# A gated mix of sliding attention and a token MLP on one core: the last 96 MLP features in column tiles, gate logits on VectorE, a shorter last store, and a new order of all queues

## The chip, the cores and the metric

The kernel runs on one core of one Trainium2 chip. The metric is the device time in microseconds of one execution; lower is better. All inputs and the output are bf16 arrays in the chip's memory. The kernel uses five engines, each with an instruction queue that is worked off in order: TensorE (PE) for matrix products, ScalarE (ACT) for exponentials, the GELU and some copies, VectorE (DVE) and GpSimd (POOL) for masks and elementwise work, and SyncE (SP), which issues all transfers.

## What is computed

x has 2048 tokens of 512 channels. The result mixes two branches by a gate of each token. Branch A is attention with 32 heads of 16 channels, in which a token sees itself and the 255 tokens before it. Branch B normalises each token and then mixes along the *tokens*: 2048 tokens to 1376 features, GELU, and back.

```python
g = sigmoid((x * gate_w).sum(-1, keepdims=True))
# A
qkv = (x @ wqkv).reshape(B, S, 3, H, Dh).transpose(2, 0, 3, 1, 4)
scores = einsum("bhqd,bhkd->bhqk", q, k) * (Dh ** -0.5)
mask = (idx[:, None] - idx[None, :] >= 0) & (idx[:, None] - idx[None, :] < 256)
p = softmax(where(mask, scores, -1e9))
a = einsum("bhqk,bhkd->bhqd", p, v).transpose(0, 2, 1, 3).reshape(B, S, D) @ wo
# B
h = layernorm(x)
u = gelu(einsum("bsd,sf->bdf", h, w1) + b1)
b = (einsum("bdf,fs->bds", u, w2) + b2).transpose(0, 2, 1)
return g * a + (1 - g) * b
```

## The kernel before

**Tiling.** Tokens are cut in 16 tiles of 128 (index `t_`) and 4 blocks of 512 (`i`). The kernel is a list of small tasks; each has a name, the engines that can run it, its dependencies, and the buffers that it takes. The names are what the text uses:

- `xtaI.n.g` transposes the first block of x on TensorE (the other three blocks, `xt1` to `xt3`, come transposed by transfer), `xtc` copies the result out.
- `qK_I`, `kK_I`, `vT` are the projections. Each is a chain of matmuls of 512 columns into one of eight banks of PSUM, the memory that TensorE writes; a name with `.0`, `.2` and so on is a pair of matmuls of the chain. `qc`, `kc`, `vc` copy the results out; `qc` multiplies with a parity pattern.
- `sJ.vN`, `sJ.C` are scores of a group of query tokens J into two pairs of banks, `eJ...` the exponentials of them on ScalarE (1024 columns each), `mJ...` the masks on VectorE or GpSimd, `pvJ.N` the products with V, `n1` to `n4` and `nz` the normalisation, which also brings the result back in place of x.
- `bs`, `ba`, `pow`, `h` are the layer norm.
- `uF.N` (F from 0 to 10) is the first half of the MLP: chain F makes 128 features for all 512 channels, with w1 as the weights and h as the 512 moving columns, over 16 token tiles. Chain 10 has the last 96 features. `ubF` adds the bias and copies to `ug`. `gelu` is one task of four instructions over all of `ug`, with two table loads of ScalarE around it.
- `yT.N` is the second half of the MLP plus the attention's output product: 11 matmuls with w2 and 4 with wo into the same bank, 15 in a chain. `fT` scales with 1 - g and adds the bias, `oT` stores. wo's product lands in the same sum since the attention result is scaled by the gate's ratio beforehand. Token tile 15 is cut in two halves of 256 columns, `y15l` and `y15r`, each with an `f` and an `o`.
- `gate0` makes the gate logits of tokens 0 to 511 on TensorE, 16 matmuls with one moving column; `glT` makes the logits of one of the other twelve token tiles on VectorE, with gate_w spread over all partitions (loaded by `gw`). `gatem`, `gatee`, `ez` finish them.

**Order.** Nothing is scheduled by a rule at run time. `PLAN` (L189) lists for each engine the task names in the order of its queue, with the numbers of the buffers taken behind the colon. `arrange` (L85) walks through the lists with costs of its own and fixes from them in which tiling the plain chains run: a chain task is "flexible" (`flex`), and takes 32-column tiles (mode p, four matmuls in place of one, on four column groups of the array at once) or the whole array (mode d), whichever `THEN` (L280) names for the stretch after the last task with a tiling of its own. Scores use row tiles (s), corner scores (c) and some products (h) 64-row or 64-column tiles, the products with V column tiles (p). A change of mode costs TensorE time, so the plan gathers tasks of a mode.

**Lines.** All flexible chains record their matmuls on L670 in `chain` (L653): with w1 and h it is u, with XT and wqkv a projection, with ug and w2 (`wb`) or with wo it is y. L942, L998 and L1042 are scores, L1087 the products with V, L894 the exponentials, L536 masks on GpSimd, L907 and L974 masks on VectorE, L754 the Q copies, L602 and L603 other copies, L802 the gate's matmuls, L822 the logits on VectorE, L438 to L441 `affine`, the eviction of u and y, L1253 and L1255 the GELU, L591 the warm-up of TensorE on zeros, L608 the transposes of x, L1305 the stores. `wb` holds w1 first and w2 later.

Of the kernel before, what the change touches and what calls it, by code (L numbers as in the profile page):

```python
# [78 lines left out]
SWITCH = 0.095  # L79

BLOCK, AHEAD, FETCH, BUSY = 256, 80, 3.6, 3.0
LATENCY = {"PE": 0.22, "ACT": 0.15, "DVE": 0.12, "POOL": 0.15, "SP": 2.0}


def arrange(tasks):  # L85
# [21 lines left out]
    while len(order) < len(tasks):  # L107
# [19 lines left out]
        t.cost = t.engines[e]  # L127
        ins = t.ins
        if e == "PE":
            new = then if t.flex else t.mode  # L130
            if new != mode:
                t.cost += SWITCH
            if t.flex and new == "p":
                t.tiled = True
                ins *= 4
            if t.mode != "d":
                then = "p" if t.name in THEN else "d"
            mode = new
# [52 lines left out]
        warm:3 xta0.0.0:7 xta0.0.1:6 warmb xta0.1.1:4 xta0.1.0:5 q1_0.0:2 k3_0.0:3 k1_0.0:6 q3_0.0:1 k0_0.0:7  # L191
        q3_0.1 q0_0.0:0 k3_0.1 q1_0.1 q1_0.2 k1_0.1 k3_0.2 k0_0.1 q0_0.1 q2_0.0:5 q1_0.3 q0_0.2 q1_0.4 q0_0.3
        k3_0.3 q3_0.2 q0_0.4 k3_0.4 q3_0.3 k2_0.0:4 q2_0.1 k0_0.2 k1_0.2 k1_0.3 k0_0.3 k1_0.4 q2_0.2 q3_0.4 q2_0.3
        k0_0.4 k2_0.1 k2_0.2 k2_0.3 k2_0.4 q2_0.4 s0.v0:62 q3_1.0:0 q3_1.2 k3_1.0:1 k3_1.2 q0_1.0:7 s0.C:42 v1.0:6
        q0_1.2 s-1.C:02 v1.2 v2.0:5 v2.2 s1.v3:02 biast:4 v0.0:7 v0.2 v3.0:5 v3.2 q1_1.0:4 s1.v0:62 v5.0:1 q1_1.2
        gate0:5 v5.2 v14.0:0 s0.v1:62 v13.0:5 k2_1.0:1 v14.2 pv-1.0:6 v10.0:4 k2_1.2 v13.2 s1.v2:26 k2_2.0:0 v10.2
        v15.0:1 v12.0:5 v12.2 v15.2 k2_2.2 pv0.0:2 pv0.1 s1.v1:64 pv0.2 v4.0:1 v4.2 k3_2.0:0 k3_2.2 s2.v1:26 v7.0:5
        v7.2 k0_2.0:4 s1.C:60 k0_2.2 v6.0:3 v6.2 s2.v3:06 k0_1.0:2 k0_1.2 k1_1.0:5 k1_1.2 pv1.0:6 pv1.1 pv1.2
        s2.v0:02 v11.0:4 v11.2 v8.0:5 v8.2 pv1.3 pv1.4 s2.v2:20 q2_1.0:5 v9.0:4 q2_1.2 s2.C:26 v9.2 k1_2.0:1 k1_2.2
        u3.0:0 u3.2 s3.v1:64 u3.4 u3.6 u3.8 s3.C:26 u3.10 u3.12 u3.14 u2.0:1 s3.v2:24 pv2.0:6 pv2.1 u7.0:0 pv2.2  # L200
        pv2.3 u7.2 u2.2 s3.v0:42 u2.4 u7.4 u7.6 s3.v3:46 u7.8 u7.10 u7.12 s4.v0:62 u2.6 u2.8 u2.10 u2.12 u2.14
        s4.v1:24 pv3.0:6 pv3.1 pv3.2 pv3.3 u7.14 u10.0:1 u10.2 s5.v2:42 u10.4 u10.6 u10.8 s4.v3:62 u10.10 q0_2.0:0
# [86 lines left out]
def kernel(  # L289
# [929 lines left out]
    for j in range(-1, NT):  # L1219
# [153 lines left out]
```

## Time and profile before

| | |
|---|---|
| time of the runs, us | 199.88, 200.21, 200.73 (median 200.21) |
| the profiled execution, us | 199.82, of which the span of its instructions 198.1 |
| TensorE matmuls, busy | 193.0 us, 4058 matmuls |
| ScalarE, VectorE, GpSimd busy | 169.0, 156.5, 80.0 us |
| granted TensorE clock | 1.00 |
| transfers | 22.02 MB, 111 GB/s on average |

The profile lists instructions with start, length, engine, line, and the tiles written and read (out<-in); `128*32` are the rows and columns of the array that a matmul uses, `128x512` the partitions and elements of its moving operand. A matmul's length holds its latency, and matmuls are pipelined, so the time that TensorE spends on one is read from its start to the next one's start. The number in brackets is the idle time just before, with what ended it. "PEq" and "SPq" are the sequencers, which issue. A transfer's landing is later than its issue.

### The profile page before, as it was taken

Reading aid. Unit: us, or ns where it says so; the run is one execution under the profiler, and the core shown is the slowest. Engines: PE = TensorE matmul, PEld = TensorE weight load, DVE = VectorE, ACT = ScalarE, POOL = GpSimd, SP = SyncE. Lnnn points to the kernel's source line nnn. Section 1 sums busy time; section 2 is a strip of 40 time slices with the busy share of each in tenths; the row PEclk is TensorE's granted clock in tenths of the full one; section 3 lists DMA queues with packets and bytes.
Section 4 is the critical chain, followed back from the end, with each engine's and each line's share of the span. In section 5 each row is a group of like instructions: output and inputs, shape, how many; then the busy total and the mean of one; then the engine's idle time right before and its main releaser. Section 6 shows DMA issues by size and latency. Waiting matters only on the chain. (4 is left out here: it accounts for less than half of the span.)

```text
span 198.1 us, 9100 instructions
## 1 busy us (share of the span) xinstructions
PE 193.0 (97%) x4058; PEld 93.3 (47%) x4058; DVE 156.5 (79%) x318; ACT 169.0 (85%) x198; POOL 80.0 (40%) x118
## 2 busy tenths in 40 slices
PE   7999999999999999999999999999999999999993
PEld 3643444353635445446543554344445354554572
DVE  1799888879998988986589799636867868869683
ACT  2369999999988996998999899899899989898632
POOL 6394897525344440214223200045069335452310
PEclk9999999999999999999999999999999999999999
DMA  5999798970060000001399770000211220200002
GB/s 156 294 284 232 131 319 278 346 187 0 8 174 18 18 0 3 3 5 32 98 364 367 280 210 3 26 26 30 68 37 58 60 68 22 62 30 30 30 3 83
DMA packets 23189, 22.02 MB, mean 111 GB/s; under 512 B 7566, under 2 KB 21262, under 8 KB 23150
## 3 DMA queue, kind: packets, MB, share of 16 engines
q1 hardware_dynamic: 23150, 21.44, 36.9%
q8 instruction: 32, 0.52, 1.1%
q14 instruction: 7, 0.06, 0.1%
HBM read 15.61 MB, written 2.10 MB: 89 GB/s over the span
## 5 line engine op out<-in xcount | busy, mean ns | idle before, releaser
L894 ACT ACTIVATE et<-ps 128x1024 bf16<-128x1024 f32 (+1 forms) x94 | 89.3, 1015 | 6.1 <-PE ps L942 2.4
L536 POOL TENSOR_SCALAR_AFFINE_SELECT et<-et 128x512 bf16<-128x512 bf16 (+2 forms) x63 | 46.7, 751 | 56.0 <-ACT et L894 40.9
L894 ACT ACTIVATE XT<-ps 128x1024 bf16<-128x1024 f32 (+1 forms) x60 | 58.1, 1011 | 7.3 <-PE ps L942 4.3
L670 PEld LDWEIGHTS <-wb 128*32 128x32 bf16 (+4 forms) x645 | 32.0, 97 | 34.5 <-issue 6.5
L670 PE MATMUL pb<-ug,wb 128*32 128x512 bf16 (+4 forms) x385 | 45.5, 366 | 0.0
L670 PE MATMUL pb<-h,wb 128*128 128x512 bf16 (+2 forms) x260 | 44.5, 381 | 0.0
L536 POOL TENSOR_SCALAR_AFFINE_SELECT XT<-XT 128x512 bf16<-128x512 bf16 (+1 forms) x28 | 20.0, 720 | 46.3 <-ACT XT L894 27.4
L670 PE MATMUL pb<-XT,wqkv 128*128 128x512 bf16 (+2 forms) x190 | 32.4, 372 | 0.4 <-DMA wqkv<-in_A_wqkv_dram 0.3
L1178 DVE STREAM_TRANSPOSE et<-ps 128x1024 f32<-128x1024 f32 (+1 forms) x17 | 20.1, 1183 | 11.9 <-PE ps L1087 11.1
L1087 PEld LDWEIGHTS <-VA 128*32 128x32 bf16 (+1 forms) x1056 | 20.1, 97 | 6.6 <-issue 1.5
L942 PE MATMUL ps<-QZ,KT 32*128 32x256 bf16 (+1 forms) x496 | 23.1, 265 | 0.0
L754 DVE TENSOR_TENSOR QZ<-pb,par 128x1024 bf16<-128x1024 f32 x16 | 19.5, 1221 | 3.2 <-PE pb L670 3.2
L670 PEld LDWEIGHTS <-wqkv 128*128 128x128 bf16 (+1 forms) x190 | 12.7, 98 | 14.6 <-DMA wqkv<-in_A_wqkv_dram 0.5
L670 PE MATMUL pb<-wo,xo 128*32 128x512 bf16 (+2 forms) x152 | 18.1, 375 | 0.0
L1087 PE MATMUL ps<-et,VA 128*32 128x128 bf16 (+2 forms) x624 | 17.9, 218 | 0.0
L942 PEld LDWEIGHTS <-KT 32*128 32x128 bf16 x496 | 7.4, 92 | 20.6 <-ACT et L894 10.7
L670 PE MATMUL pb<-wqkv,XT 128*128 128x512 bf16 (+1 forms) x70 | 16.5, 381 | 0.0
L974 DVE TENSOR_TENSOR et<-et,mask 128x512 bf16<-128x512 bf16 x26 | 13.3, 510 | 2.5 <-ACT et L894 2.4
L441 DVE TENSOR_SCALAR ot<-pb,c,c 128x512 bf16<-128x512 f32 (+1 forms) x11 | 8.6, 785 | 7.4 <-PE pb L670 7.3
L1087 PE MATMUL ps<-XT,VA 128*32 128x128 bf16 (+2 forms) x432 | 13.9, 215 | 0.0
L1087 PEld LDWEIGHTS <-VZ 128*32 128x32 bf16 x832 | 13.2, 98 | 0.7
L770 DVE BATCH_NORM_STATS2 stats<-xo 128x6 f32<-128x512 bf16 x16 | 10.7, 682 | 3.1 <-DMA xo<-in_A_x_dram 3.1
(76 smaller groups left out, 199.4 us busy)
## 6 DMA issues: line engine op xcount, KB each, us to landing
wb<-in_B_w_dram SPq DMA_DIRECT2D x8, 512.0 KB, 8.2
wb<-in_B_w_dram SPq DMA_DIRECT2D x2, 2048.0 KB, 9.2
VZ<-VA SPq DMA_DIRECT2D x26, 70.0 KB, 3.0
xo<-in_A_x_dram SPq DMA_DIRECT2D x3, 512.0 KB, 5.5
out_dram<-ot SPq DMA_DIRECT2D x12, 128.0 KB, 2.4
wb<-in_B_w_dram SPq DMA_DIRECT2D x4, 352.0 KB, 5.8
wqkv<-in_A_wqkv_dram SPq DMA_DIRECT2D x4, 256.0 KB, 5.0
wb<-in_B_w_dram SPq DMA_DIRECT2D x1, 1024.0 KB, 5.3
```

The lines of the kernel that those rows point to most:

```text
L441: return nc.vector.tensor_scalar(out=out_, in0=in_, scalar1=scale, scalar2=bias, op0=ALU.mult, op1=ALU.add)
L536: return nc.gpsimd.affine_select(out=out_, in_=in_, pattern=[[0, n] for n in pattern] + [[step, HB]], compare_op=op, fill=0.0, base=base_, ...
L670: made.append(nc.tensor.matmul(buf(b)[c:z_, c0:c0 + w_], lhsT=lhsT[:, c:z_], rhs=rhs, start=(j == 0), stop=(j == n - 1), skip_group_check= ...
L754: lambda k=k, b=b: nc.vector.tensor_tensor(out=QZ[:, k, :, (i % NQ) * SB:(i % NQ + 1) * SB], in0=buf(b)[:, None, :].to_broadcast([P, 2, SB ...
L770: f"bs{t_}", {"DVE": 0.67}, lambda b=b, t_=t_: nc.vector.bn_stats(buf(b)[:], xo[:, t_, :]),
L894: lambda e=e, b=b, shape=shape: nc.scalar.activation(out=shape(buf(e)), in_=shape(buf(b)), func=ACT.Exp, scale=SCALE),
L942: made.append(nc.tensor.matmul(to[:, :, done:done + m], lhsT=keys(j if x == "A" else j - 1, k)[rows], rhs=q[rows], start=True, stop=True, ...
L974: made.append(nc.vector.tensor_tensor(out=v, in0=v, in1=m.to_broadcast(list(v.shape)), op=ALU.mult))
L1087: return lambda: nc.tensor.matmul(to(), lhsT=v() if callable(v) else v, rhs=buf(e)[rows, col:col + n], start=first, stop=last, tile_positi ...
L1178: lambda: nc.vector.transpose(out=view(buf(tr).bitcast(FP32)), in_=view(buf(o))), [last], takes=[tr], uses=[o],
```

## The change

Five things change together:

1. The last 96 features (chain 10 of u) no longer go through `chain` but through a new function, `narrow`. Of the four column groups of 32, three make 32 features each for 384 of the 512 channels; the fourth makes the remaining 128 channels for all three feature groups, one after the other, next to each other in its part of the bank. The eviction becomes `ub10` (384 columns) and `uc10` (three pieces of 32 partitions by 128).
2. The gate logits of tokens 0 to 511 are made on VectorE as the others are (`NGP` from 1 to 0): `gate0` goes, `gl0` to `gl3` come, and `gw` is loaded earlier.
3. The last token tile is cut in 256, 128 and 128 columns (`y15l`, `y15r`, `y15m`).
4. The zeros of the warm-up are 128 columns, spread by a broadcast read.
5. `arrange` has other costs, and all five lists of `PLAN` and `THEN` are new. The lists are cut here to the stretches that the text speaks of.

```diff
@@ -76,10 +76,29 @@
         self.ready = 0.0
 
 
-SWITCH = 0.095
-
-BLOCK, AHEAD, FETCH, BUSY = 256, 80, 3.6, 3.0
-LATENCY = {"PE": 0.22, "ACT": 0.15, "DVE": 0.12, "POOL": 0.15, "SP": 2.0}
+TURN = {
+    "d": dict(d=0, s=0.100, p=0.100, c=0.098, h=0.100),
+    "s": dict(d=0.116, s=0, p=0.115, c=0.105, h=0.114),
+    "p": dict(d=0.134, s=0.116, p=0, c=0.110, h=0.130),
+    "c": dict(d=0.149, s=0.137, p=0.146, c=0, h=0.137),
+    "h": dict(d=0.150, s=0.137, p=0.135, c=0.140, h=0),
+}
+
+BLOCK, AHEAD, FETCH, BUSY = 256, 80, 3.1, 3.5
+LATENCY = {"PE": 0.21, "ACT": 0.15, "DVE": 0.11, "POOL": 0.12, "SP": 2.0}
+
+
+def cost_of(t, e):
+    c, n = t.engines[e], t.name
+    if e == "PE":
+        return c - 0.02 if t.mode == "s" else c * 0.738 if t.mode == "c" else c
+    if e == "DVE":
+        return max(0.1, c - 0.06)
+    if e == "ACT":
+        return c - 0.085 if n[:2] in ("vc", "kc", "ub") else c - 0.008 if n[0] == "e" else c
+    if e == "POOL" and n[0] == "m" and ".C" in n:
+        return c * 1.14
+    return c
 
 
 def arrange(tasks):
@@ -124,15 +143,15 @@
         assert best is not None, "no task can start: " + ", ".join(q[head[e]].name for e, q in queue.items() if head[e] < len(q))
         start, e, t = best
         head[e] += 1
-        t.cost = t.engines[e]
+        t.cost = cost_of(t, e)
         ins = t.ins
         if e == "PE":
             new = then if t.flex else t.mode
-            if new != mode:
-                t.cost += SWITCH
+            t.cost += TURN[mode][new]
             if t.flex and new == "p":
                 t.tiled = True
                 ins *= 4
+                t.cost += 0.0025 * t.ins
             if t.mode != "d":
                 then = "p" if t.name in THEN else "d"
             mode = new
@@ -188,100 +207,107 @@
...
-        warm:3 xta0.0.0:7 xta0.0.1:6 warmb xta0.1.1:4 xta0.1.0:5 q1_0.0:2 k3_0.0:3 k1_0.0:6 q3_0.0:1 k0_0.0:7
...
-        gate0:5 v5.2 v14.0:0 s0.v1:62 v13.0:5 k2_1.0:1 v14.2 pv-1.0:6 v10.0:4 k2_1.2 v13.2 s1.v2:26 k2_2.0:0 v10.2
...
-        s4.v1:24 pv3.0:6 pv3.1 pv3.2 pv3.3 u7.14 u10.0:1 u10.2 s5.v2:42 u10.4 u10.6 u10.8 s4.v3:62 u10.10 q0_2.0:0
...
-        u9.6 u9.8 s8.v0:04 u8.10 u9.10 u9.12 u8.12 u8.14 s8.v2:06 pv7.0:4 u9.14 pv7.1 pv7.2 pv7.3 s10.v0:02
...
-        q2_3.2 y0.0:7 y0.2 y0.4 y8.0:2 y0.6 y4.2 y0.8 s9.v1:40 y4.4 y8.2 y0.10 y8.4 y0.11 y0.13 s9.v3:40 y4.6 y4.8
...
-        y15l.2 y15r.0:6 y15l.4 y15l.6 y13.10 pv15.0:4 y14.10 pv15.1 pv15.2 y15r.2 y15l.8 y15l.10 y15r.4 y13.11
-        y14.11 y14.13 y13.13 y15r.6 y15r.8 y15l.11 y15l.13 y15r.10 y15r.11 y15r.13
...
-        const zeros bs3:1 xtc0.0.0 bs2:0 ba3 parity bs1:1 ba2 ba1 bs0:0 ba0 qc1_0 bs4:1 qc0_0 ba4 qc3_0 qc2_0 qc3_1
...
-        x0.0 x0.2 wqk0 wqk1 wqk2 wqk3 x1.4 xt1 wv x2.8 bias xt3 x3.12 xt2 vs0 w1_02 w1_03 vs1 w1_22 vs2 gw w1_12
-        w1_23 w1_01 w1_00 w1_10 w1_11 vz2:0 w1_13 vz3:1 vz4:2 vz5:0 w1_20 w1_21 vz6:1 vz8:0 w2_0 vz7:2 w2_1 w2_2
-        vz9:1 wo o0 o4 o8 o7 vz10:2 vs13 o2 o9 o1 vz11:0 vz12:1 o5 o10 vz13:2 o11 vz14:0 o3 o6 o12 o14 o13 o15l
...
+        warm:5 xta0.0.1:4 xta0.0.0:7 warmb xta0.1.0:3 k0_0.0:7 k2_0.0:5 k1_0.0:0 q0_0.0:1 xta0.1.1:4
...
+        q3_1.0:1 q3_1.2 s0.C:26 k2_1.0:0 k2_1.2 v5.0:4 s-1.C:26 v14.0:5 v14.2 v5.2 s1.v3:02 v2.0:6 biast:7
...
+        pv3.2 u0.0:4 u0.2 u2.14 pv3.3 s5.v2:26 u0.4 u10.0:5 u10.2 u10.4 s4.v3:02 u10.6 u10.8 u10.10 u10.12
+        s4.v2:06 u10.14 u0.6 u0.8 s4.C:20 u0.10 u0.12 u0.14 q3_2.0:0 q3_2.2 s6.v0:62 q0_2.0:1 q0_2.2 pv4.0:4
...
+        u8.8 u9.0:6 s8.v1:02 u9.2 u9.4 u9.6 s8.v0:24 u8.10 u8.12 u8.14 s8.v2:04 u9.8 pv7.0:2 u9.10 u9.12
+        q1_3.0:7 u9.14 pv7.1 s10.v0:04 q1_3.2 k2_3.0:6 k2_3.2 pv7.2 pv8.0:4 pv8.1 pv8.2 pv8.3 pv7.3 q3_3.0:0
+        q2_3.0:7 k0_3.0:1 k0_3.2 q3_3.2 q2_3.2 s9.v1:24 y0.0:6 y0.2 y0.4 y0.6 y0.8 y4.0:7 y4.2 y4.4 y4.6
+        s9.v3:04 y4.8 y0.10 y0.11 y0.13 s9.v2:42 y4.10 y4.11 y4.13 y2.0:6 s9.C:40 y2.2 y2.4 y2.6 s9.v0:02
...
+        y14.2 y14.4 y14.6 y14.8 pv15.0:0 pv15.1 pv15.2 y15l.0:2 y13.11 y13.13 y15l.2 y15r.0:3 y15l.4 y15l.6
+        y14.10 y15r.2 y14.11 y14.13 y15l.8 y15l.10 y15l.11 y15r.4 y15l.13 y15r.6 y15r.8 y15r.10 y15m.0:0
+        y15r.11 y15r.13 y15m.2 y15m.4 y15m.6 y15m.8 y15m.10 y15m.11 y15m.13
...
+        zeros const bs1:0 xtc0.0.1 ba1 parity bs3:1 xtc0.1.0 xtc0.1.1 ba3 bs2:0 bs0:1 qc0_0 ba0 ba2 gl1
+        qc1_0 bs6:1 gl0 h3 qc2_0 qc3_0 gl2 gl3 qc3_1 gatem0 ba6 bs4:0 ez0 bs5:1 ba4 biasc bs7:0 ba5 ba7
...
+        x0.0 x0.2 wqk0 wqk1 wqk2 wqk3 gw x1.4 wv xt1 xt3 bias x2.8 xt2 vs0 x3.12 w1_02 vs1 w1_00 w1_11 w1_03
+        vz6:1 vz3:0 vz2:2 vs2 w1_12 w1_10 w1_01 w1_20 w1_13 wo vz4:2 w1_21 w1_23 w1_22 vz7:0 vz5:2 vz8:2
+        w2_0 w2_1 vz11:1 w2_2 o4 vz9:0 o0 o8 vz10:2 o2 o9 o10 o7 vz14:2 vz13:1 vz12:0 vs13 o11 o3 o5 o6 o1
...
@@ -316,7 +342,7 @@
     EPS = 1e-5
     SCALE = DH ** -0.5
     NPE = 1
-    NGP = 1
+    NGP = 0
     NQ = 2
     NK = 3
 
@@ -360,7 +386,7 @@
     ez = sb.tile([P, NT], FP32, name="ez")
 
     EZ = sb.tile([P, 4 * NT], FP32, name="EZ")
-    zeros = ug[:, 0, :]
+    zeros = ug[:, 0, 0:P]
     ident = sb.tile([P, P], BF16, name="ident")
     mask = sb.tile([P, 7, HB], BF16, name="mask")
     par = sb.tile([P, 2], FP32, name="par")
@@ -515,7 +541,7 @@
         nc.vector.memset(half[:], -0.5)
         nc.vector.memset(biases[:], 0.0)
 
-    kz = add("zeros", {"DVE": 0.25}, lambda: nc.vector.memset(zeros, 0.0))
+    kz = add("zeros", {"DVE": 0.16}, lambda: nc.vector.memset(zeros, 0.0))
     k0 = add("const", {"DVE": 0.25}, set_constants)
 
     def identity():
@@ -588,7 +614,10 @@
 
     def warming(n, w):
         return [
-            nc.tensor.matmul(buf(wu)[:, 0:w], lhsT=zeros[:, 0:P], rhs=zeros[:, 0:w], start=True, stop=True)
+            nc.tensor.matmul(
+                buf(wu)[:, 0:w].rearrange("p (a b) -> p a b", b=P), lhsT=zeros,
+                rhs=zeros[:, None, :].to_broadcast([P, w // P, P]), start=True, stop=True,
+            )
             for _ in range(n)
         ]
 
@@ -1232,6 +1261,34 @@
 
 
 
+    NW = 3 * D // 4
+
+    def narrow(fc, mms, deps):
+        b = bank("u")
+        last = None
+        for a in range(0, NT, 2):
+            def emit(a=a):
+                made = []
+                for j in range(a, a + 2):
+                    w, r, rows = mms[j]
+                    for c in range(0, rows, 32):
+                        made.append(nc.tensor.matmul(
+                            buf(b)[c:c + 32, 0:NW], lhsT=w[:, c:c + 32], rhs=r[:, 0:NW], start=(j == 0),
+                            stop=(j == NT - 1), skip_group_check=True, tile_position=(0, c),
+                        ))
+                    for c in range(0, rows, 32):
+                        made.append(nc.tensor.matmul(
+                            buf(b)[rows:P, 4 * c:4 * c + D - NW], lhsT=w[:, c:c + 32], rhs=r[:, NW:D],
+                            start=(j == 0 and c == 0), stop=(j == NT - 1), skip_group_check=True,
+                            tile_position=(0, rows),
+                        ))
+                return made
+            last = add(
+                f"u{fc}.{a}", {"PE": 0.34}, emit, list(deps) if last is None else [last],
+                takes=[b] if a == 0 else [], uses=[] if a == 0 else [b], mode="p", ins=24,
+            )
+        return b, last
+
     ub = []
     m1 = []
     for fc in range(NFC):
@@ -1239,13 +1296,28 @@
         fsz = min(P, F - f0)
         g, w0 = fc // 4, (fc % 4) * P
         mms = [(w1[g][:, t_, w0:w0 + fsz], h[:, t_, :], fsz) for t_ in range(NT)]
-        b, t = chain(f"u{fc}", mms, dw1[g] + hready, "u")
+        if fsz == P:
+            b, t = chain(f"u{fc}", mms, dw1[g] + hready, "u")
+        else:
+            b, t = narrow(fc, mms, dw1[g] + hready)
         m1.append(t)
+        w_ = D if fsz == P else NW
         ub.append(add(
-            f"ub{fc}", {"ACT": 0.66, "DVE": 0.745},
-            lambda b=b, fsz=fsz, fc=fc: affine(ug[:fsz, fc, :], buf(b)[:fsz, :], None, b1c[:fsz, fc:fc + 1]),
+            f"ub{fc}", {"ACT": 0.18 + 0.00094 * w_, "DVE": 0.21 + 0.00104 * w_},
+            lambda b=b, fsz=fsz, fc=fc, w_=w_: affine(
+                ug[:fsz, fc, 0:w_], buf(b)[:fsz, 0:w_], None, b1c[:fsz, fc:fc + 1]
+            ),
             [t, k3], uses=[b],
         ))
+        if fsz < P:
+            def emit_rest(b=b, fc=fc):
+                return [
+                    affine(
+                        ug[c:c + 32, fc, NW:D], buf(b)[fsz:P, 4 * c:4 * c + D - NW], None, b1c[c:c + 32, fc:fc + 1]
+                    )
+                    for c in range(0, fsz, 32)
+                ]
+            ub.append(add(f"uc{fc}", {"ACT": 0.93, "DVE": 0.9}, emit_rest, [t, k3], uses=[b]))
 
     cuts = [(0, 3), (3, 7), (7, NFC - 1)]
 
@@ -1255,7 +1327,7 @@
         made.append(nc.scalar.activation(ug[:rows, NFC - 1, :], ug[:rows, NFC - 1, :], ACT.Gelu_apprx_tanh))
         return made
 
-    gelu = add("gelu", {"ACT": 8.3}, emit_gelu, ub)
+    gelu = add("gelu", {"ACT": 7.0}, emit_gelu, ub)
     gelu_at = [1.3 + 0.15 + 0.43 * (3 if fc < 3 else 7 if fc < 7 else fc + 1) + 0.12 * (1 + (fc >= 3) + (fc >= 7)) + 0.2 for fc in range(NFC)]
 
     def gates():
@@ -1279,7 +1351,7 @@
 
     for t_ in range(NT):
 
-        parts = [("", 0, D)] if t_ < NT - 1 else [("l", 0, D // 2), ("r", D // 2, D)]
+        parts = [("", 0, D)] if t_ < NT - 1 else [("l", 0, D // 2), ("m", D // 2, 3 * D // 4), ("r", 3 * D // 4, D)]
         for tag, c0, c1_ in parts:
             mms = []
             for fc in range(NFC):
```

## The prediction

> **What bounds the kernel now.** The page's first part and the waits of TensorE's matmul queue, in the profiled execution (span 198.1 us):
>
> ```profile
> PE 193.0 (97%) x4058; PEld 93.3 (47%) x4058; DVE 156.5 (79%) x318; ACT 169.0 (85%) x198; POOL 80.0 (40%) x118
> ...
> PE pb L591 <- DVE ug L518: 1.4, 1, 1.4
> PE pb L670 <- DMA wqkv<-in_A_wqkv_dram: 0.3, 1, 0.3
> PE pb L670 <- ACT XT L894: 0.2, 1, 0.2
> ```
>
> The reader is to see a TensorE that works from 1.4 us to 195.0 us and has two waits over 0.1 us after its start. So the time is the sum of what TensorE issues, and I read every price from start to start in its timeline. First the stretch with the last 96 features (128*96 in the rows):
>
> ```profile
> 62.63 1.47 PE L670 MATMUL pb<-h,wb 128*128 128x512 bf16 x6
> 64.04 0.40 PE L942 MATMUL ps<-QZ,KT 32*128 32x256 bf16 x8
> 64.36 1.50 PE L670 MATMUL pb<-h,wb 128*96 128x512 bf16 x6
> 65.79 0.40 PE L942 MATMUL ps<-QZ,KT 32*128 32x256 bf16 x8
> 66.12 0.63 PE L670 MATMUL pb<-h,wb 128*96 128x512 bf16 x2
> ```
>
> Six matmuls of 512 columns take 1.41 us to the next start: 6 x 0.216, and some 0.1 for the change to another tiling of the array. Over all 169 changes in this execution, leaving the untiled mode costs 0.095, leaving column tiles 0.104, and entering any mode 0.010. 96 rows of weights cost as much as 128. Column tiles with 128 columns each, and the gate's matmuls:
>
> ```profile
> 31.21 0.41 PE L1087 MATMUL ps<-et,VA 128*32 128x128 bf16 x16
> 31.45 0.40 PE L1087 MATMUL ps<-XT,VA 128*32 128x128 bf16 x16
> ...
> 23.02 0.54 PE L802 MATMUL pb<-gwc,XT 128*128 128x1 bf16 x16
> 23.43 0.81 PE L670 MATMUL pb<-wqkv,XT 128*128 128x512 bf16 x3
> ```
>
> Sixteen tiled matmuls take 0.235, with the entry: four rounds of four, 0.056 each, new weights for every one. The gate takes 0.41. Then the head and the tail:
>
> ```profile
> 5.26 1.06 PE L608 MATMUL pb<-ident,xo 128*128 128x128 bf16 x8
> 6.57 2.61 PE L670 MATMUL pb<-XT,wqkv 128*128 128x256 bf16 x17 [0.26 <-DMA wqkv<-in_A_wqkv_dram]
> ...
> 193.62 0.81 DVE L441 TENSOR_SCALAR ot<-pb,c,c 128x512 bf16<-128x512 f32 x1 [0.25 <-PE pb L670]
> ...
> 195.04 0.55 DVE L441 TENSOR_SCALAR ot<-pb,c,c 128x256 bf16<-128x256 f32 x1 [0.61 <-PE pb L670]
> ...
> 195.61 0.33 SPq L1305 DMA_DIRECT2D out_dram<-ot  x1
> ```
>
> The first projection starts when wqkv's first block lands (6.57), whatever stands before it. The tail is one eviction, one store, and the end at 198.1. Last, ScalarE around the GELU, where its queue is closed to exponentials:
>
> ```profile
> 111.56 3.88 ACT L894 ACTIVATE XT<-ps 128x1024 bf16<-128x1024 f32 x4 [0.83 <-ACT ez L837]
> 115.47 1.28 ACT L1253 ACT_TABLE_LOAD   x1
> 116.76 4.66 ACT L1253 ACTIVATE ug<-ug 128x1536 bf16<-128x1536 bf16 x3
> ...
> 121.96 1.28 ACT L894 ACT_TABLE_LOAD   x1
> 123.55 1.94 ACT L894 ACTIVATE et<-ps 128x1024 bf16<-128x1024 f32 x2 [0.31 <-PE ps L942]
> ```
>
> From the first table load to the end of the second 7.77 us pass; a following exponential is done about 1.03 later.
>
> **The change, part by part.**
> *Gate on VectorE.* Sixteen matmuls go: -0.40, all on TensorE's path. VectorE gets four logit pairs more, 0.695 + 0.081 each by their rows, some 2.9 us, at about 10 to 18 us into the kernel, between the Q products that s0 to s1 wait for. For it the gate vector's load moves up to just behind the four wqkv loads on SP's queue, past x1, wv, the three transposes and the biases: 128 KB more ahead of each of them. Cover: the fourth wqkv block is in use at 9.02, and the gate vector follows it with half a block's bytes, so by about 9.5; the first logit is due after Q's first product, past 10.5. Cover gone, every us of delay holds VectorE's in-order queue, and s0 behind it.
>
> *u10 in column tiles.* Before: 8 pairs at 0.432 = 3.46. After, per token tile three column tiles run 384 columns (0.216 x 384/512 = 0.162) while the fourth runs three times 128 columns (3 x 0.056 = 0.168): 16 x 0.168 = 2.69, so -0.77. No row of before has unequal widths side by side. Ends: 2.59 if the 384 columns alone count (16 x 0.162), and 5.28 if the 384 and the three 128s follow each other (16 x 0.330). I take 2.69, because the nearest row, the sixteen tiled matmuls, shows four tiles each pacing itself at 0.056 with fresh weights. The eviction becomes one of 384 columns and three of 32 x 128 on VectorE, some 0.6 + 3 x 0.3, beside TensorE.
> The Trainium skill ("TensorE: Matmul & The Clock Gate", Part 3, The mechanism) speaks against it: weight loads overlap running matmuls only where the row groups differ, and these tiles all use every row. With its load time (P/1.2 ns, 27 ns for 32 columns; same page, LDWEIGHTS) my estimate would be 0.056 + 0.027 three times, 0.249 per token tile and 3.98 in all, a loss of 0.5. The sixteen matmuls above have full rows too, and would then take 0.33 where 0.225 was measured, so the row decides. The same section says that matmuls end in the order of issue, which no run here shows for unequal widths.
>
> *Order.* Counted off the two programs' TensorE queues, mode changes go from 169 to 167 in other kinds; priced by kind: -0.24. Tiled and untiled pairs cost the same (0.432), so which pairs are tiled is free. SP's queue is new too. Three blocks of w1's last group, two before, now stand behind vz4, which waits for pv2; before, the two were issued at 55.41 to 56.6 and served u10 at 63.08. One more is 352 KB, 1.2 us at the early 290 GB/s, and u10 stands 1.5 us later: covered. vz9 moves behind o4, the first store, to some 128 us; VZ lands 3.0 us after its issue by the page, and pv9 follows past 135. Gone, such a cover costs its delay in full, since TensorE waits in order.
>
> *Last piece of 128 columns.* Fifteen matmuls more for the same columns: a 256-column pair took 0.218 where half of a 512 pair is 0.216, so some 0.003 each: +0.05. The last eviction shrinks from 0.545 by the slope of the two rows ((0.81 - 0.545)/2): -0.13. The store has half the bytes: 128 KB stores landed in 2.4 us, the 64 KB one in 1.5, so between 0 and -0.4. I take -0.12 (smaller rows), -0.25 with the eviction. The third store on SP is covered: its issue (0.33) ends during the last 0.7 us of matmuls.
>
> *Head.* The zeros are filled first, so the warm-up starts some 0.3 us sooner; it ends before x lands at 3.74 and gains nothing. The last four transposes (0.43 at the early half rate, 0.107 each) move behind the first four projections, past 6.57: there they cost 0.22 at full rate. What left the stretch before 6.57 only lengthens the wait there.
>
> TensorE from the first projection on: -0.40 - 0.77 - 0.24 + 0.05 + 0.22 = -1.14.
>
> *Waits.* After 6.57 before had some 0.8 us beyond the prices: 0.16 while the clock was half (two starts 0.19 apart, then 0.109), 0.33 at 113 to 114.5 (a bank held by the last exponentials), 0.13 at 143, 0.07 at 145, small ones. In the new order s9.v1 is issued within the GELU and s9.v3 stands 10.57 us of TensorE work behind s10.v0's end; ScalarE needs 0.2 to take up the score (before: scores issued by 123.33, exponential at 123.55), then 2 x 0.97 + 7.77 + 1.03, in all 10.94, until the bank is free: +0.37 there. In exchange the first y stands 7.47 us of work behind the last u, where 6.61 were before, so the 0.33 should go. ScalarE's own queue from the first exponential to the GELU grows from 117 to 122 instructions (four K copies and two evictions more, one V copy less): 91.8 to 94.7 us at the back-to-back pace of each kind, in 99.1, now 98.4, us of TensorE work between the same points. Its slack falls from 7.3 to 3.7 us; for that I add +0.2. VectorE gets fifteen masks from GpSimd and ends near 164 us, GpSimd near 68: neither fills the span. Waits: +0.25, between -0.5 and +1.5.
>
> Sum: -1.14 - 0.25 + 0.25 = -1.14. On the profiled execution's 199.82 (198.1 of span and 1.7 around it) that is 198.7; that execution lay 0.39 under the median of the runs shown, 200.21, from which I count: **199.1 us**.
>
> **Rivals.**
> (1) *ScalarE becomes the bound before the GELU.* For: its slack halves, and each score task waits for a bank that an exponential frees. Against: 3.7 us stay, and before lost under 0.5 us there. If a third of it is missing at the wrong places, +1.1: 200.2.
> (2) *Unequal widths don't run side by side*, slower than before: the 128s queue behind the 384s, 5.28 instead of 2.69, +2.6: 201.7. For: no row shows it. Against: the even rows. It decides from 0.60 per pair of token tiles on (0.336 + 2.1/8 brings 201.2); 0.336 is forecast.
> (3) *A load lands late.* The new order wants the fourth block of transposed x at about 18.8 us, before at 23.86, and before it landed at 17.97. For: under 1 us of cover. Against: 512 KB of x now come after it and only 128 KB more before it, which at the early 290 GB/s is 1.3 us sooner. 1 us late: 200.1.
>
> **How the numbers follow.** Under 0.5% (1.0 us) a measurement here can't tell from no change, so the borders are 199.2 and 201.2. Forecast 0.60 (its own range 198.3 to 199.9; 0.42 of it under 199.2, 0.18 above); (1) 0.20, 0.18 of it within; (2) 0.15, 0.14 of it slower; (3) 0.05, 0.04 within. That is 0.42 faster, 0.41 the same, 0.17 slower. The range goes from 198.2, where the waits of before vanish too, to 201.0, past (1) and (3), leaving most of (2) out.
>
> **What will show it.** In the profile after: 128*32 matmuls of 384 columns from h and wb, with about 0.168 from one token tile's first to the next's (0.33 is rival 2); no L802-like 128x1 matmuls; one entry for the wait at 6.57; a TensorE idle time near 120 us of under 0.5; the score matmuls' waits on ScalarE before 110 us under 1 us in sum (rival 1 if above); no wait on XT near 19 us; a last eviction of some 0.41. I am wrong if TensorE's sum from 6.57 on doesn't fall by about 1.1, or if idle time eats it.

## The result: slower, and the profile after

The changed kernel takes 204.95 us (median; 203.86 to 206.12), the kernel before in the same comparison 200.47 (199.88 to 201.06). The ratio is 1.024, interval 1.021 to 1.028: slower by 2.4%, where 199.1 us was forecast. The profiled execution took 204.35, with a span of 202.6; it is compared below with the 199.82 and 198.1 of before.

The work itself came out as the sum said. Lines in the changed kernel lie some 26 to 29 further on: L699 has the flexible chains, L1071 the corner scores, L1116 the products with V, L1275 and L1280 the narrow chain, L467 an eviction. From the page's first part and from the timeline of TensorE and VectorE, after:

```profile
PE 192.4 (95%) x4047; PEld 93.5 (46%) x4047; DVE 156.6 (77%) x343; ACT 169.9 (84%) x200; POOL 63.2 (31%) x100
...
66.08 0.33 PE L1275 MATMUL pb<-h,wb 128*32 128x384 bf16 x3
66.09 0.33 PE L1280 MATMUL pb<-h,wb 128*32 128x128 bf16 x3
66.24 0.35 PE L1275 MATMUL pb<-h,wb 128*32 128x384 bf16 x3
...
199.85 0.41 DVE L467 TENSOR_SCALAR junk<-pb,c,c 128x128 bf16<-128x128 f32 x1 [0.86 <-PE pb L699]
```

TensorE is busy 0.6 us less. A token tile of the narrow chain follows the last one after 0.16 us (66.08 to 66.24), and the last eviction takes 0.41. But the span is 4.5 us longer, so TensorE must have waited. Its waits, after (us in total, times, longest):

```profile
PE ps L1116 <- issue: 2.0, 1, 2.0
PE pb L617 <- DVE ug L544: 1.0, 1, 1.0
PE pb L699 <- issue: 1.0, 1, 1.0
PE ps L1071 <- issue: 1.0, 1, 1.0
PE pb L699 <- DMA wqkv<-in_A_wqkv_dram: 0.9, 1, 0.9
PE ps L1116 <- DMA VS<-VA: 0.6, 1, 0.6
```

Three waits are put down to "issue": nothing that the profile shows held TensorE there. Before had none. Where they are, in TensorE's timeline after:

```profile
98.82 0.37 PE L1071 MATMUL ps<-QZ,KT 32*64 32x128 bf16 x22
100.18 0.30 PE L1071 MATMUL ps<-QZ,KT 32*64 32x128 bf16 x10 [0.99 <-issue]
...
117.10 0.41 PE L1116 MATMUL ps<-XT,VA 128*32 128x128 bf16 x16
119.53 0.24 PE L1116 MATMUL ps<-et,VA 128*32 128x128 bf16 x4 [2.02 <-issue]
...
183.75 0.43 PE L1071 MATMUL ps<-QZ,KT 32*64 32x128 bf16 x32
185.22 0.38 PE L699 MATMUL pb<-ug,wb 96*128 96x512 bf16 x1 [1.04 <-issue]
```

The first breaks a group of 32 matmuls after the 22nd. All 32 belong to one task (s7.C), and in the trace only the first of them waits for a semaphore, so the 23rd was not held by missing data. By start-to-start times the three pauses cost 1.23, 2.21 and 1.11 us over their prices, in all 4.5.

The table of transfer queues of after names what is left:

```profile
q1 hardware_dynamic: 23294, 21.44, 36.2%
q8 instruction: 31, 0.51, 1.0%
q14 instruction: 7, 0.06, 0.1%
```

Queue q8 moves instructions, 31 packets in the execution, 16 KB each (0.51 MB). The trace has 8129 TensorE instructions (weight loads, matmuls, and some 35 that only handle semaphores), so a packet of q8 is a block of 256. I counted TensorE's instructions and drew a border every 256, at the offset that fits all traces (the 192nd is the first). "Spare" is the next border less the packet's end less 1.25 us:

```
after: border passed   packet            next border   spare    TensorE's pause (work resumes)
  95.67              97.99 to  98.94      98.92       -1.27      1.23  (100.18)
 114.11             117.15 to 118.13     117.24       -2.14      2.21  (119.53)
 182.26             182.85 to 183.97     183.91       -1.32      1.11  (185.22)
 before, smallest of 31 borders: -0.04;  every other border of after: -0.37 or more
```

The places agree to the instruction. Counted from 0, the last one before each of the three pauses is number 3776, 4544 and 7360, which is 192 plus 14, 17 and 28 times 256; the four pauses in the other two traces that have pauses and lack no matmul record (experiment 7 and the repeat of experiment 3) lie on such numbers too.

This fits a block that is asked for when the one before it begins to be used. Its packet starts 0.8 us after that (median of the 170 borders after 120 us in all runs), takes 1.0, and its instructions run 1.25 us later at the earliest (1.4 in the median of the larger pauses): some 3 us. If TensorE issues 256 instructions faster, it stops. The 0.8 is no constant: 21 of the 170 packets started up to 1.1 us before TensorE passed the border and 18 more than 1.6 us after it, 15 of these behind a block that was late itself. A plain pair of 0.43 us is 4 instructions, the same pair in column tiles 16. The packets at 97.99 and 117.15 started 2.3 and 3.0 us after their borders: the first load of w2 had been issued at 95.59, the two pieces of the third at 112.80 and 114.10.

What remains is known waits. pv1.4 lost 0.77 at 41.3, since vs2 now stands behind vz6, vz3 and vz2 on SP's queue. The first block's last projections and the first V chain lost 0.8, at 12.4 to 16.6, where the first transposed block of x (xt1) landed at 16.61 (12.05 before): on SP's queue gw (128 KB) and wv (512 KB) now stand ahead of it.

The ratios below leave out executions more than 1.5% above a kernel's fastest, so medians with their range stand beside them.

### The profile page after: what moved, and what is told of

The parts are those of the page before. It is cut to its first block, busy times and chain, and to the rows that moved or that the text cites. A ratio compares the mean times of both kernels' runs of the same rounds, so it can differ in the third digit from the quotient of the medians.

```text
span 202.6 us, 9055 instructions
## 1 busy us (share of the span) xinstructions
PE 192.4 (95%) x4047; PEld 93.5 (46%) x4047; DVE 156.6 (77%) x343; ACT 169.9 (84%) x200; POOL 63.2 (31%) x100
## 4 chain that ended last, share of the span: by engine, by line
PE 80%; DMA 6%; SPq 5%; ACT 5%; issue 3%; DVE 0%; DVEq 0%
PE pb L699 56%; PE ps L1116 10%; PE ps L971 9%; DMA XT<-in_A_x_dram 5%; PE ps L1071 3%; ACT et L923 3%; SPq L758 1%; DMA VS<-VA 1%; SPq L496 1%; PE pb L1280 1%; SPq L757 1%; ACT KT L631 1%; ACT VA L631 1%; SPq L480 1%; PE pb L1275 1%
## 5 line engine op out<-in xcount | busy, mean ns | idle before, releaser
L923 ACT ACTIVATE et<-ps 128x1024 bf16<-128x1024 f32 (+1 forms) x107 | 100.6, 1001 | 12.1 <-PE ps L971 7.3
L562 POOL TENSOR_SCALAR_AFFINE_SELECT et<-et 128x512 bf16<-128x512 bf16 (+3 forms) x51 | 34.9, 698 | 77.0 <-ACT et L923 54.1
L923 ACT ACTIVATE XT<-ps 128x1024 bf16<-128x1024 f32 x47 | 46.8, 1040 | 3.0 <-PE ps L971 1.6
L699 PEld LDWEIGHTS <-wb 128*32 128x32 bf16 (+2 forms) x646 | 30.9, 97 | 34.1 <-issue 6.7
L699 PE MATMUL pb<-ug,wb 128*128 128x512 bf16 (+4 forms) x288 | 44.8, 364 | 1.0 <-issue 1.0
L699 PE MATMUL pb<-h,wb 128*32 128x512 bf16 (+1 forms) x358 | 40.4, 381 | 0.0
L699 PE MATMUL pb<-XT,wqkv 128*128 128x512 bf16 (+2 forms) x154 | 31.9, 369 | 1.0 <-DMA wqkv<-in_A_wqkv_dram 0.9
L562 POOL TENSOR_SCALAR_AFFINE_SELECT XT<-XT 128x512 bf16<-128x512 bf16 (+1 forms) x22 | 15.6, 712 | 41.1 <-ACT XT L923 17.2
L1116 PEld LDWEIGHTS <-VA 128*32 128x32 bf16 (+1 forms) x1056 | 20.0, 97 | 9.3 <-issue 4.1
L1116 PE MATMUL ps<-et,VA 128*32 128x128 bf16 (+2 forms) x736 | 20.6, 216 | 2.0 <-issue 2.0
L699 PEld LDWEIGHTS <-wqkv 128*128 128x128 bf16 (+1 forms) x154 | 11.8, 97 | 14.7 <-issue 2.7
L699 PE MATMUL pb<-wo,xo 128*128 128x512 bf16 (+3 forms) x102 | 17.6, 363 | 0.0
L699 PE MATMUL pb<-wqkv,XT 128*128 128x512 bf16 x64 | 16.5, 380 | 0.0
L936 DVE TENSOR_TENSOR et<-et,mask 128x1024 bf16<-128x1024 bf16 (+1 forms) x23 | 14.6, 651 | 2.3 <-ACT et L923 2.3
L467 DVE TENSOR_SCALAR ot<-pb,c,c 128x512 bf16<-128x512 f32 (+1 forms) x12 | 9.4, 783 | 5.7 <-PE pb L699 5.6
L1116 PEld LDWEIGHTS <-VZ 128*32 128x32 bf16 x832 | 13.2, 97 | 0.7
```

Of the source, the lines that this page charges most:

```text
L467: return nc.vector.tensor_scalar(out=out_, in0=in_, scalar1=scale, scalar2=bias, op0=ALU.mult, op1=ALU.add)
L562: return nc.gpsimd.affine_select(out=out_, in_=in_, pattern=[[0, n] for n in pattern] + [[step, HB]], compare_op=op, fill=0.0, base=base_, ...
L699: made.append(nc.tensor.matmul(buf(b)[c:z_, c0:c0 + w_], lhsT=lhsT[:, c:z_], rhs=rhs, start=(j == 0), stop=(j == n - 1), skip_group_check= ...
L923: lambda e=e, b=b, shape=shape: nc.scalar.activation(out=shape(buf(e)), in_=shape(buf(b)), func=ACT.Exp, scale=SCALE),
L936: return nc.vector.tensor_tensor(out=v, in0=v, in1=m[:, None, :].to_broadcast([P, n, w]), op=ALU.mult)
L1116: return lambda: nc.tensor.matmul(to(), lhsT=v() if callable(v) else v, rhs=buf(e)[rows, col:col + n], start=first, stop=last, tile_positi ...
```

## Experiments

**1. Other borders, same work.** The kernel before, with its warm-up on zeros cut finer.

```diff
-    add("warm", {"PE": 2.2}, lambda: warming(5, 512), [kz], takes=[wu], ins=10)
+    add("warm", {"PE": 2.2}, lambda: warming(51, 50, 32), [kz], takes=[wu], ins=102)
```

> The kernel before with one edit: the warm-up on zeros ahead of the first transposes is cut into 51 matmuls of 50 columns (32 columns of weights) in place of 5 of 512, that is the same number of columns and 92 TensorE instructions more, all before 4 us. From the first projection on nothing differs. Theory (TensorE's instructions come in blocks of 256; a block is asked for when the one before it begins to be used up, and is usable some 2.9 us later, 2 us more beside a load of w2): the 92 instructions shift every block border against the work, and the borders fall worse; expected stalls of 1.0 at 95, 3.0 at 114, 1.2 at 155, 1.1 at 175 and 0.9 at 185, together +5 to +8 us, about 207. Rival (the loss of the changed kernel comes from its own order, waits and transfers): no instruction of the real work differs, so 200.4, within 0.5 either way.

210.14 us (208.78 to 211.92), ratio 1.047 (1.042 to 1.052). The profiled execution is the longest, 211.92. The warm-up took the same 2.31 us, and the first projection started 0.3 us earlier than before, at 6.25. TensorE's waits and one place of its timeline (L673, L945 and L1090 are L670, L942 and L1087 of before):

```profile
PE pb L673 <- issue: 7.2, 22, 3.3
PE ps L1090 <- issue: 3.2, 3, 1.4
...
115.32 0.40 PE L945 MATMUL ps<-QZ,KT 32*128 32x256 bf16 x8
119.07 1.23 PE L673 MATMUL pb<-XT,wqkv 128*128 128x512 bf16 x3 [3.35 <-issue]
```

Of the 22 waits in the first line 20 are 0.16 us each: the trace lacks the records of 32 matmuls, and a missing one looks like a short wait. Against before, task by task, the pauses are 0.74 at 45.5, 1.19 at 96.2, 2.94 at 115.3, 1.62 at 157.7, 1.51 at 178.3, 1.11 at 189.0 and 0.66 at 202; the spare at these borders is -0.51, -1.05, -3.28, -1.45, -1.38, -1.15 and -0.66. Five were forecast, all five came. 46 matmuls on zeros, done before 4 us, cost the kernel before 10 us: the pauses belong to the count, not to the new order. The rival falls for the kernel before; for the changed one the count at its pauses (above) says the same. The total was above the forecast because of the two small pauses and, in this execution, because the clock fell after the long one (last section).

**2. The narrow chain alone**, in the kernel before.

```diff
-        b, t = chain(f"u{fc}", mms, dw1[g] + hready, "u")
+        if fsz == P:
+            b, t = chain(f"u{fc}", mms, dw1[g] + hready, "u")
+        else:
+            b, t = narrow(fc, mms, dw1[g] + hready)
...
-        q3_2.2 s4.C:06 u0.2 u0.4
+        q3_2.2 u0.2 u0.4 s4.C:06
...
-        qc0_2 n31:1 n32:0 qc3_2
+        qc0_2 uc10 n31:1 n32:0 qc3_2
```

> The kernel before with the column tiles for the last 96 features alone (its second eviction on VectorE behind the second q0 copy, and the corner scores s4.C two tasks later, because they take the bank that this eviction frees). 160 TensorE instructions more from 63 us on. By the forecast's sum the narrow chain is worth -0.8 us. Theory of the instruction blocks: the 160 instructions also shift the borders, with stalls of 0.7 at 63.6, 0.5 at 94, 0.9 at 140, 0.9 at 163, 0.5 at 180 and 1.1 at 188, so +4.6-0.8 = +3 to +4.5 us, about 204. Rival (the part is what the forecast said and the loss lies elsewhere in the new order): 199.6.

207.32 us (206.69 to 209.81), ratio 1.034 (1.031 to 1.038). Pauses of 0.74 at 65, 1.31 at 97, 1.33 at 143, 1.13 at 167, 0.53 at 173, 0.84 at 177, 0.56 at 186 and 1.16 at 194: the six places forecast (each later by the pauses before it) and two more. They are read in the longest execution, 209.81; some 0.6 us of it is a wait on an exponential at 74, which the moved s4.C makes (experiment 3). The part that was to bring 0.8 us costs 7 when its 160 instructions move the borders.

**3. Both at once**, 92 + 160 = 252 instructions from the narrow chain on.

> Both edits at once: column tiles for the last 96 features, and the warm-up in 51 matmuls. From the end of the narrow chain on the shift is 92+160 = 252 instructions, 4 short of one whole block, and before it the shift of 92 costs nothing (the first border that it spoils lies at 95 us). Theory of the instruction blocks: two edits that each cost 3 us or more cancel, and only the gain of the narrow chain is left: 199.2 to 200, faster than before by 0.5 to 0.9. Rival (each edit costs by itself, or neither does): the sum of the two other runs' differences, +9 us and more by their theory, or -0.8 with both of the others near the kernel before.

> The run with both edits (column tiles and 51 warm-up matmuls) once more, unchanged, for its spread: four executions took 201.0, 204.7, 204.7 and 207.1. If the spread belongs to this kernel's thin margins, the executions again lie between 200.8 and 207; if it was that one chip or minute, they lie within 1 us of 201.

204.67 us (200.96, 204.66, 204.68 and 207.11; too far apart for a ratio), and in the repeat 203.60 (202.73 to 204.19), ratio 1.016 (1.013 to 1.019). Two edits that cost 10 and 7 us alone cost 4.4 and 3.4 together, so they do cancel in large part, but not to the forecast. The profiled execution of 200.96 has one pause, 1.17 at 44.5, and 0.6 from s6.v0 waiting for a bank that my move of s4.C held. The repeat's has that pause, with 0.8, and another of 1.78 at 95.5. There the same instructions met a packet that started 3.17 us after its border, where it had been 0.77. So the spread belongs to the kernel: its spares are small, and the packet's lag is not the same each time. What delayed it in the repeat the trace doesn't show.

**4. The late transfer.** The changed kernel with one SP entry moved.

```diff
-        vz6:1 vz3:0 vz2:2 vs2 w1_12
+        vs2 vz6:1 vz3:0 vz2:2 w1_12
```

> The changed kernel with one transfer moved: the copy of the third group's values (vs2) is issued ahead of the three copies vz6, vz3 and vz2, which it stood behind. In the changed kernel TensorE waits 0.77 us at pv1.4 for it. Expected: that wait goes, pv1.4 starts on time, and 204.3 becomes 203.6; the three pauses at 99, 117 and 184 us stay, since they hang on the count of instructions and not on this transfer. Rival (the pauses follow from late transfers in some way): more than 1.5 us gained, or the pauses gone.

204.24 (203.79 to 206.77), ratio 1.023 (1.016 to 1.029). The step of pv1.4, wait and work, went from 1.01 to 0.24. The three pauses stay, at 97.5, 116.1 and 183.4, with 1.50, 2.54 and 1.02 us, and a small one of 0.5 joined at 64. Fixing it gave 0.6 us on the profile; it is not where the time went.

**5. Sixteen instructions fewer** in the changed kernel, with experiment 4's entry moved. Four of them lie ahead of the pause at 98, all 16 ahead of that at 184.

```diff
 THEN:
-    s6.v1 s8.v2
...
-    add("warm", {"PE": 2.2}, lambda: warming(5, 512), ...
+    add("warm", {"PE": 2.2}, lambda: warming(9, 256), ...
```

> The changed kernel with vs2 ahead of vz6, and 16 TensorE instructions taken out of the stretch ahead of the pauses: the pairs k3_3.0 and u9.8 are no longer cut into column tiles (12 instructions each less), and the warm-up is 9 matmuls of 256 columns in place of 5 of 512 (8 more). No order changes, and the work is the same. Theory of the instruction blocks: the borders move, and of the three pauses the ones at 98 us (1.5 in the last run) and 184 us (1.0) go, while the one in pv8 at 117 us (2.5) stays, because there the pv tasks use up a block in less than 3 us whatever the phase: 204.1 becomes 201.3 to 201.8. Rival (untiling two pairs out of 56 is no real change): 204, all three pauses in their places.

202.35 (200.71 to 207.39; 10 executions), ratio 1.010 (1.006 to 1.014). The profiled execution, 200.71, has one wait on issue over 0.2 us left:

```profile
PE pb L699 <- issue: 3.5, 22, 0.2
PE ps L1116 <- issue: 1.8, 1, 1.8
...
97.66 0.43 PE L1071 MATMUL ps<-QZ,KT 32*64 32x128 bf16 x32
98.02 0.61 PE L699 MATMUL pb<-h,wb 128*128 128x512 bf16 x2
```

The first line is 22 waits of under 0.2 behind score tasks, where the starts stay at the prices of before; this trace lacks 33 matmul records, and the complete one of experiment 7 has no such line. The reader is to see that the pauses at 98 and 184 are gone, while that in pv8 stays (2.0, spare -2.05), as forecast. At 184 this is the count: the block before the pause was used up in 1.65 us in experiment 4 and lasts 3.41 here. At 98 it is not. There the block lasts 3.21 us, 3.26 in experiment 4, but its packet started 0.89 us after the border, where it had been 2.43. So this half of the forecast came true by luck, and the pause was to come back (experiment 7). The gain was 3 us in this execution; the median, with its spread, 1.9 against experiment 4.

**6. Sparse work in front of pv8**, on top of experiment 5.

```diff
-        pv7.2 pv8.0:4 pv8.1 pv8.2 pv8.3 pv7.3 q3_3.0:0 q2_3.0:7 k0_3.0:1 k0_3.2 q3_3.2 q2_3.2 s9.v1:24
+        pv7.2 pv7.3 q3_3.0:0 q2_3.0:7 k0_3.0:1 k0_3.2 q3_3.2 q2_3.2 pv8.0:4 pv8.1 pv8.2 pv8.3 s9.v1:24
```

> As two_untiled, and six pairs of the last chunk's projections and pv7.3, which stand behind pv8, are moved ahead of pv8.0, so that 2.6 us of work with few instructions lies between the request of the block and its first use. Theory of the instruction blocks: the last pause goes too, and TensorE waits for no block any more: 199.0 to 199.8, faster than the kernel before by 0.2 to 0.7%. Rival (the changed kernel's own order costs time beside the pauses): 201 or more, with other waits in place of the pause.

204.22 (201.74 to 210.87, 4 executions, no ratio). No pause is left (smallest spare 0.00), and the forecast missed all the same: the time became a wait that my own move made, from TensorE's waits,

```profile
PE ps L971 <- DVE XT L1207: 2.7, 1, 2.7
```

s9.v1 now stands behind pv8 and needs the banks of pv7 and pv8, which VectorE clears one after the other, 1.2 us each, from 118.97 on.

**7. That wait taken away**, on top of experiment 6. So that the count at later borders stays, pv8.3 also leaves `THEN`.

```diff
-        pv8.3 s9.v1:24 y0.0:6 y0.2 y0.4 y0.6 y0.8 y4.0:7 y4.2 y4.4
+        pv8.3 y0.0:6 y0.2 y4.0:7 y0.4 y4.2 s9.v1:24 y0.6 y0.8 y4.4
...
-        n18:8 n17:g kc2_3 n28 n27 qc2_3 kc0_3
+        n17:g kc2_3 n27 qc2_3 n18:8 n28 kc0_3
...
 THEN:
-    pv8.3
```

> As mended, with the wait that its moved tasks made taken away: in mended s9.v1 stood straight behind pv8 and waited 2.7 us for VectorE to clear the banks of pv7 and pv8. Here five pairs of the second half (y0.0, y0.2, y4.0, y0.4, y4.2) go ahead of s9.v1, and VectorE clears pv7, which ends 3 us before pv8, first. The count of TensorE instructions at every later border is that of mended. Theory of the instruction blocks, with this wait as the only other loss: 200.0-2.7 = 197.3 to 197.8 of span, 199.0 to 199.6 in its good executions, so 0.2 to 0.6% under the kernel before; the spread from one execution to the next stays about 2 us or more, because borders at 54, 65 and 90 us have only 0 to 0.3 us to spare. Rival (the changed kernel is limited by ScalarE or by the second half's order once TensorE runs ahead): 200.5 or more, with waits on ScalarE at s9 to s11.

202.93 (201.30 to 203.86, and one execution of 468.66 that left no trace), ratio 1.011 (1.008 to 1.014). The wait for VectorE went, but a pause was back at s7.C, in work that was not touched, now after 24 matmuls, since four instructions fewer stand before it than in the changed kernel; it is the same border, number 3776:

```profile
98.00 0.37 PE L1071 MATMUL ps<-QZ,KT 32*64 32x128 bf16 x24
100.17 0.26 PE L1071 MATMUL ps<-QZ,KT 32*64 32x128 bf16 x8 [1.80 <-issue]
```

Both traces side by side, with the first load of w2:

```
                 border   block's packet   w2 issued   its first packets   spare
mended            94.39      95.21           94.29          95.6            0.26
mended_late_s9    94.87      97.80           94.77          95.8           -1.83
```

In mended the block's packet slipped in 0.4 us ahead of the load's first packets. In mended_late_s9 the border fell 0.5 us later, the load's first packets 0.2 us later, and the block's packet came 2.0 us into the load. These distances alone don't settle who comes first: in experiment 5 the load's first packets came 0.97 us after the border, as here (0.96), and in the changed kernel (0.96) and experiment 4 (0.97); the block came first in experiment 5 alone.

**8. The load held back** until the block has been asked for, on top of experiment 7.

```diff
-        dw2.append(add(f"w2_{g}", ..., emit, m1[4 * g:4 * g + 4], lat=2.5))
+        behind = [t for t in tasks if t.name == "pv6.3" and g == 0]
+        dw2.append(add(f"w2_{g}", ..., emit, m1[4 * g:4 * g + 4] + behind, lat=2.5))
...
+            if t.name == "w2_0":
+                tc.add_manual_dep(first, hold.name, ...)
```

> As mended_late_s9, with one wait added: the first load of w2 on SyncE's queue waits for pv6.3, which is some 1.5 us later than it goes now. Nothing else moves. In mended the block for s7.C was fetched at 95.2 us, just ahead of that load's first packets at 95.5, and s7.C ran through; in mended_late_s9, where all was 0.4 us later, the load's packets came first, the block started at 97.8, and TensorE paused 2.0 us at s7.C. Theory (a race between the block and the load): with the load behind it the block starts at 95.7, the pause at s7.C goes in every execution, and 202.9 becomes 199.4 to 200.8, spread 2 us. Rival (the lag of that block is chance and has nothing to do with the load): the median stays at 202.5 or more, or the pause at s7.C stays in the profile.

200.46 (199.07 to 202.44; 12 executions), ratio 1.002 (0.999 to 1.005): 2.5 us under experiment 7, as the theory said, and the same as the kernel before. The profiled execution took 199.07 (span 197.4), 0.75 under that of before; the waits of its TensorE over 0.2 us are all in the head, and s7.C runs through:

```profile
PE pb L699 <- issue: 3.5, 22, 0.2
PE pb L617 <- DVE ug L544: 1.0, 1, 1.0
PE pb L699 <- DMA wqkv<-in_A_wqkv_dram: 1.0, 1, 1.0
PE pb L637 <- DMA xo<-in_A_x_dram: 0.5, 1, 0.5
...
97.57 0.43 PE L1071 MATMUL ps<-QZ,KT 32*64 32x128 bf16 x32
97.93 0.60 PE L699 MATMUL pb<-h,wb 128*128 128x512 bf16 x2
```

The block's packet started at 95.29 and the load was issued at 95.54. The forecast held for the median; the spread is 3.4 us and not 2. That holding the load back helps is shown for this place only. And with no pause left in its profile, the median is still 1.4 us above the 199.1 of the forecast; what the other executions lose, one trace doesn't show.

**9. The kernel before with the narrow chain and borders chosen for it**: s6.v0 two tasks later, 29 warm-up matmuls, and 31 of the stretches of flexible pairs switched between tiled and untiled.

> The kernel before with column tiles for the last 96 features, s6.v0 three tasks later (in the run with both edits it waited 0.7 us for its bank), the warm-up in 29 matmuls of 88 columns, and another choice of the pairs that are cut into column tiles (31 of the 84 groups switched), chosen so that every block border has at least 0.3 us to spare by the lags seen in the traces. Theory of the instruction blocks: no pause of more than 0.3 us, the narrow chain's 0.85 us and some 0.3 us of fewer mode switches are kept: 198.7 to 199.4. Rival (the margins vary from one execution to the next by more than that, as the spread from 201.0 to 207.1 in the run with both edits may say): 200 to 204 with a spread of 2 us or more.

201.18 (200.41 to 202.18; 10 executions), ratio 1.006 (1.004 to 1.009). The border at 40 us has a spare of -0.36 and that at 161 one of -0.41, with pauses of 0.3 and 0.5; the other pauses are gone. The spread is 1.8 us, not the 2 or more of the rival, but the gain isn't there either: in this order s4.C needs the bank that the narrow chain's second eviction frees, and behind it pv4.0 waited 0.5 us on an exponential; 0.7 more were lost at 19 us to VectorE.

## Why the prediction was wrong, by its steps

*The step that failed: "Waits: +0.25, between -0.5 and +1.5".* Beyond the prices TensorE idled 1.05 us after 6.57 in the forecast and 6.6 us in the profile. 4.5 of the difference are the three pauses. The list of waits had loads, banks, ScalarE and VectorE, each found by asking who holds a buffer, and nothing for the instructions themselves. Experiments 1 and 2 show that term by making it, experiment 5 (at 184) and experiment 8 by taking it away.

*"Tiled and untiled pairs cost the same, so which pairs are tiled is free"* is true of the price (0.432) and false of the count: 4 instructions or 16. This sentence shut the door on the right answer. The diff had the clue, the constants `BLOCK`, `AHEAD`, `FETCH` and `BUSY` of `arrange` (256, 80, and 3.1 and 3.5 us in place of 3.6 and 3.0), and I read past them. The page had it too: q8 stands in its table of queues. The Trainium skill ("Runtime: NRT & Kernel Launch", Instruction fetch mechanics) says that instructions are fetched in 16 KiB blocks of 256, the next while the current one runs, and that crossing a border is mostly hidden. The traces agree on block and order. They differ on hidden: at 256 instructions in under 3 us it isn't, and the changed kernel lost 4.5 us. By the page's sentence the forecast would not have changed; the measurement decides.

*u10, -0.77.* A pair took 0.325 (0.336 forecast), so rival 2 falls, with its condition of 0.60. The chain's gain is some 0.85 on TensorE's path. The rule that the prediction weighed and set aside, that weight loads overlap only between different row groups, would have given 0.249 per token tile; 0.162 was measured.

*Gate, order, last piece, head: together -0.37 forecast.* They gave some 0.2 beside u10: idle time aside, TensorE's stretch from the first projection to its last matmul took 1.05 us less (186.6 against 187.6), where -1.14 was forecast for all of it. The first projection started at 6.55 (6.57). The tail is 2.85 us (3.11 before), the forecast -0.25.

*Waits that were priced.* Rival 1: the waits on ScalarE are 0.2 us in sum, so it falls. The +0.37 at s9.v3 can't be judged in after, where TensorE came there 3.4 us late. Rival 3 had the right kind and not the right place. The block that it named, xt3, landed at 18.70 (17.97 before), just in time. Late came xt1, 0.8 us: the prediction put 128 KB more ahead of it, and wv's 512 KB had moved there too. Late came vs2 behind the vz copies, 0.77 us, although w1, gw and vz9 had been followed past each queue entry. A small slip beside the path: the four logits are 3.1 us by their rows (4 x 0.776), not 2.9.

*The range* ended at 201.0, because no case held a wait that the profile of before doesn't show. Before has none of this kind since its 31 borders all fall well: the smallest spare is -0.04 us, three more are below 0.25. Experiment 1 shows how little that takes to lose.

## What to carry to other kernels

Count instructions as well as time: where TensorE's next 256 instructions are issued in less than the some 3 us that the block after them takes (5 to 6 us in the median beside w2's loads), it stops, and any edit upstream that changes the count moves the place. A wait that the profile puts down to "issue" in the middle of equal instructions can be this; look then at the packets of the instruction queue. When a part that should gain loses by more than its own size, shift the count without changing the work before judging the part.

## What the runs showed of the hardware that was not expected

- A block is late beside a big load. Borders passed between 96 and 114 us, while w2's loads run, saw the packet start after 1.4 to 4.5 us (median of 33: 3.4), later ones after 0.8. Experiment 8 points to the load as the cause for one border (its median fell by 2.5 us); for the others only the coincidence is shown. Two packets started 3.0 us after their borders with no transfer under way (125.6 in the changed kernel, 124.8 in experiment 4), which stays open.
- A pause can be paid twice. In experiment 1 TensorE was idle 3.35 us until 119.07; pairs then took 0.85 in place of 0.43, and 1.7 us more were gone. In experiment 7, after 1.80 us, the granted clock was 0.64 on average from 100 to 104. In both the trace's clock record has 0.5 for 3.41 us and then 1.00 again. After the 2.02 us of the changed kernel it stayed at 1.00. Experiment 1 by windows (busy us of TensorE, weight loads, VectorE, ScalarE, GpSimd; granted clock; transfers):

```profile
115.00:119.00 4.00, 0.72 (x52) 0.50 (x38) 2.89 (x9) 3.97 (x4) 1.27 (x2) 1.00 0.97 302
119.00:123.00 4.00, 3.93 (x11) 1.50 (x11) 0.69 (x1) 3.99 (x4) 0.00 (x0) 0.57 0.32 103
```

  The first line is the pause, beside a transfer at 302 GB/s; in the second TensorE is busy all the time, with 11 matmuls, at a clock of 0.57.
- Unequal tiles run side by side: three column groups with 384 columns and a fourth with three times 128, new weights for each, take 0.162 us per token tile, as much as 384 columns alone by the prediction's price (0.216 x 384/512).
- Twelve executions of one program (experiment 8) lie 3.4 us apart, where 17 of the kernel before lie 1.5 us apart. It has no pause in its profile, but three of its last borders have 0.05 to 0.17 us to spare.
